# Attention and two feed-forward layers on one core: weight tiles finished a tile earlier, and three edits in the last layer

## The chip, the core and the metric

The kernel runs as one program on one core of a Trainium2 chip. The core has a matrix engine (TensorE, in the profile PE; its weight loads are listed as PEld), a vector engine (VectorE, DVE), a scalar engine (ScalarE, ACT) and GpSimd (POOL). Each runs its own instructions strictly in the order in which they were written, and they meet at semaphores. The sync engine (SP) issues most transfers, also in order; ScalarE issues some of its own. Sixteen DMA engines carry them. SBUF is the on-chip memory, PSUM the memory that TensorE writes to. The metric is the time of one execution in microseconds (us) of the device.

## The reference, cut to what matters

```python
# q, k, v: [4, 8, 768, 64]; per head h: gamma = 1 - 2**(-5-h)
for t in range(768):
    state = gamma * state + k[t] outer v[t]
    y[t]  = q[t] @ state / 8
x  = y as [3072, 512]
h  = x @ w1_in;   g = max(0.01*h, h);             x = g @ w1_out     # first layer,  512 -> 2048 -> 512
h  = x @ w2_in;   g = h * sigmoid(1.702*h);       out = g @ w2_out   # second layer, 512 -> 2048 -> 512
```

The weights arrive as 64-bit floats. All four products are taken from operands that are split in a high and a low part, three matmuls (low x high, high x high, high x low) for each product.

## The kernel before, in words

**Stages.** (1) Attention runs in 24 steps `s` of 128 tokens. (2) The first layer works on six blocks of 512 tokens and 16 slices `m` of the hidden width: `ffn_in(blk, m)` is twelve matmuls of 512 columns, `ffn_out(blk, m)` is twelve too. `ffn_in` of block 0 is woven into the attention steps 4 to 22. After attention, `ffn_in` of block 1 is woven with `ffn_out` of block 0, which catches up by two slices for each `ffn_in` ("the ramp"); from then on the two alternate one to one. (3) The second layer computes each product in seven products of half-size blocks (Strassen's scheme in Winograd's form): `first` runs 32 pairs (block of tokens, slice `q`) of seven products each and writes the gated result to the DRAM tensor `gd`; `second` reads `gd` back, runs seven products of eight slices for each of three blocks of tokens, and turns the results with transposes on TensorE before they go out.

**A first-layer weight tile.** Each call of `work()` moves the tiles of one list (`order`: 16 tiles for `ffn_in`, then 16 for `ffn_out`) one place on: it loads the raw 64-bit words of tile n+2 (`load_raw`, three buffers), converts tile n (`convert`: two ScalarE steps on L137 and L138, four VectorE steps on L139 to L144, an addition on GpSimd on L146), and finishes tile n-1 (`finish`: `split` on L123 and L124, the high part by a copy on ScalarE, the low part by a subtraction on GpSimd, into the tile `home` or `rest`). During attention `work()` runs in steps 2 and 3 and then one step after each step with an `ffn_in`; in the ramp it runs after each `ffn_out` of block 0, and once more before the ramp. Thus tile m is finished in the call just ahead of the matmuls that use it. `ffn_in` and `ffn_out` take the high part in their first two matmuls and the low part in the third.

**What else lies on those engines.** In an attention step VectorE masks the scores (`sm`, L249), updates the state (`st`, L291) and scales the queries (`qs`, L256); GpSimd scales the keys (L260); ScalarE copies the result out (L307). In the ramp `g_split` writes the two parts of the activations of slice n+2 after `ffn_out` of slice n: a ScalarE copy (L123) that waits for the buffer of slice n, and a VectorE subtraction (L124).

**The second layer's buffers.** `first` has a pool of five tiles `g` for results that wait for their store to `gd` (issued by ScalarE, L577); four tiles are written in each pair. As slices of the first weights fall free, `after(q)` has SP load the last layer's weights (`wdo`) into the same place (L839, 1792 KB each). `prepared()` creates `Early`, which has SP load the first eight blocks of `gd` (L694, 256 KB each), three pairs before the end. In `second`, `result()` queues a turn (`turn`, eight transposes on L763, then a ScalarE copy on L767) two ticks later; a tick is one product. For the quarter C22 of the result (`other`, block row 1, column 1) GpSimd first adds two tiles (L778), and its turn uses the same PSUM tile "d" as the turn just before.

Of the kernel before, what the change touches and what calls it, by code (L numbers as in the profile page):

```python
# [13 lines left out]
I32 = mybir.dt.int32  # L14
AF = mybir.ActivationFunctionType
ALU = mybir.AluOpType
# [8 lines left out]
KF = DFF // P  # L25
# [58 lines left out]
def retention_two_ffn(ctx: ExitStack, tc: tile.TileContext, qkv, consts, small, w1i, w1o, w2i, w2o, scratch, out):  # L84
    nc = tc.nc
# [7 lines left out]
    low, low_x = ExitStack(), ExitStack()  # L93
# [21 lines left out]
    later = Later()  # L115
# [3 lines left out]
    xf, raw, conv = {}, {}, {}  # L119
# [11 lines left out]
    def convert(kind, m):  # L131


        t = raw.pop((kind, m))
        low, high = t[:, :, 0], t[:, :, 1]
        a = cv_p.tile([P, 512], U32, tag="a", name="a")
        nc.scalar.activation(out=a.bitcast(F32), in_=high.bitcast(F32), func=AF.Abs)  # L137
        nc.scalar.activation(out=low.bitcast(I32), in_=low, func=AF.Copy, scale=2.0**-29)  # L138
        nc.vector.tensor_scalar(out=high, in0=high, scalar1=0x80000000, scalar2=None, op0=ALU.bitwise_and)  # L139
        nc.vector.tensor_scalar(out=a.bitcast(F32), in0=a.bitcast(F32), scalar1=HW_MIN, scalar2=HW_MAX,  # L140
                                op0=ALU.max, op1=ALU.min)
        nc.vector.tensor_scalar(out=a, in0=a, scalar1=3, scalar2=0x40000000,
                                op0=ALU.logical_shift_left, op1=ALU.bitwise_xor)
        nc.vector.scalar_tensor_tensor(out=a, in0=a, scalar=0x7FFFFFFF, in1=high,  # L144
                                       op0=ALU.bitwise_and, op1=ALU.bitwise_or)
        nc.gpsimd.tensor_tensor(out=a.bitcast(I32), in0=a.bitcast(I32), in1=low.bitcast(I32), op=ALU.add)  # L146
        conv[kind, m] = a, t

    def finish(kind, m):

# [19 lines left out]
    W0 = 4  # L170
# [7 lines left out]
    def work():  # L178

        n = done[0]  # L180
        done[0] += 1
        if n + 2 < len(order):
            kind, m = order[n + 2]
            load_raw(kind, m, w1i if kind == "i" else w1o)
        if n < len(order):
            convert(*order[n])
        if 0 < n <= len(order):
            kind, m = order[n - 1]
            finish(kind, m)

    def ffn_in(blk, m):
        h = ps.tile([P, TB], F32, tag="h", name="h")
# [19 lines left out]
    with ExitStack() as actx:  # L212
# [124 lines left out]
        for s in range(len(steps)):  # L337
            if s == 0:
                keep_warm(6)
            elif s + 1 < len(steps):  # L340
                a_scores(s + 1)
            o = a_out(s)
            if s >= W0 - 2 and done[0] < KF + 1 and (s < W0 or now_in[s - 1]):
                work()
            a_store(s, o)
            if s == 0:
                keep_warm(4)
                a_scores(1)
                keep_warm(6)
            if s + 2 < len(steps):  # L350
                a_decay(s + 2)
            if s + 4 < len(steps):
                a_load(s + 4)
            for m in now_in[s]:
                if m == KF - 1:
                    g_split(seq[0])
                ffn_in(0, m)
# [141 lines left out]
    first2 = KF + LAG  # L499
    g_split(seq[1])  # L500
    work()
    n = 0
    for i in range(KF, len(seq)):
        ffn_in(*seq[i])
# [50 lines left out]
    def first(wt, blocks, g_p, after, prepared):  # L555


        with ExitStack() as c:
# [42 lines left out]
            state = {}  # L601
            for n in range(len(pairs) + 1):
                now = n < len(pairs)
                if n == len(pairs) - 3:
                    prepared()
                cur, old = state.setdefault(n, {}), state.pop(n - 1, None)
                last = first_ = False
# [101 lines left out]
    def second(wt, early):  # L709
        with ExitStack() as c:  # L710
# [41 lines left out]
                                         start=(new and q == 0 and m == 0), stop=(q == NQ - 1 and m == 2),  # L752
                                         skip_group_check=True)

            def result(blk, r, col, t, tag):

                rows = slice((2 * blk + r) * T2, (2 * blk + r + 1) * T2)

# [10 lines left out]
                        out=out[rows].rearrange("(b p) f -> p b f", p=P)[:, :, 2 * col * P : 2 * col * P + 2 * P],  # L769
                        in_=s.rearrange("p b j f -> p b (j f)")))  # L770

                later.at(2, turn)

            kept = {}

            def evacuate(blk, i):
# [15 lines left out]
                elif i == 6:  # L792
# [6 lines left out]

                    def other():  # L800
                        put(k, t, k, e=nc.gpsimd)
                        result(blk, 1, 1, k, "d")

                    later.at(1, other)
                elif i == 3:
# [21 lines left out]
            later.drain()  # L827

    blocks.open(left, 2)
    g_p = pool(left, "g1", 5, "left")  # L830
    for k, i in enumerate(FORMS[4:]):
        blocks.form(0, i, (k, k, k))
    for _ in range(2):
# [77 lines left out]
```

## Time and profile before

| | |
|---|---|
| median of 3 runs | 1297.26 us (1295.88 to 1297.53) |
| the profiled execution | 1292.65 us, of which the span of the profile is 1290.6 us |
| TensorE busy in the span | 1161.7 us, 90% |
| VectorE, ScalarE, GpSimd busy | 655.0, 490.7, 258.0 us |
| TensorE's granted clock, mean of the span | 0.953 of 2.4 GHz |

Times in the views are in us from the span's start. "Idle before" is the time an engine stood still ahead of an instruction, followed by what released it. The granted clock of a stretch is a mean between the two levels 1.2 GHz (0.5) and 2.4 GHz (1.0). A row with "x10" merges ten instructions that follow each other. The end of a matmul is modelled, so neighbouring matmul rows overlap by some tenths of a us.

### The profile page before, as it was taken

To read this page: it belongs to the slowest core of one execution; us is meant where nothing else is said; L and a number is where in the kernel's file an instruction comes from. 1 tells how busy PE (TensorE), PEld (TensorE's weight loads), DVE (VectorE), ACT (ScalarE), POOL (GpSimd) and SP (SyncE) were. 2 spreads that over 40 slices of the span, in tenths; PEclk is the share of its full clock that TensorE was granted. 3 is DMA by queue.
4 is the path that set the end of the run, shared out by engine and by line. 5 is a ranking of instruction groups with operands and counts; after the bars stand their busy time and mean duration, and the time that the engine had idled before them with its cause. 6 is when DMAs were issued, how large, how long until landed. Compare 5 with 4: busy or idle time off the path is not lost.

```text
span 1290.6 us, 16434 instructions
## 1 busy us (share of the span) xinstructions
PE 1161.7 (90%) x6189; PEld 963.5 (75%) x6189; DVE 655.0 (51%) x1034; ACT 490.7 (38%) x823; POOL 258.0 (20%) x269
## 2 busy tenths in 40 slices
PE   8677767656699999999999999999999699999997
PEld 5566555444488888888888889999999687887885
DVE  6344343222235554554454435666574478586683
ACT  2222223222234444444443334344342344444443
POOL 3343231322213333332233301011110000000000
PEclk9898897777799999999999999999999899999999
DMA  9475532111024445444433685343439952623421
GB/s 364 166 267 188 194 121 98 53 61 49 1 100 156 134 147 166 167 151 152 159 127 124 229 338 191 117 153 120 151 106 334 344 188 65 229 66 123 138 66 66
DMA packets 88095, 199.03 MB, mean 154 GB/s; under 512 B 7888, under 2 KB 51920, under 8 KB 82640
## 3 DMA queue, kind: packets, MB, share of 16 engines
q1 hardware_dynamic: 69584, 172.81, 38.8%
q10 hardware_dynamic: 18432, 25.17, 5.4%
q8 instruction: 48, 0.79, 0.2%
q14 instruction: 31, 0.25, 0.1%
HBM read 125.60 MB, written 72.35 MB: 153 GB/s over the span
## 4 chain that ended last, share of the span: by engine, by line
PE 79%; DMA 6%; DVE 5%; POOL 5%; issue 3%; ACT 2%; SPq 0%; POOLq 0%; ACTq 0%; DVEq 0%
PE y L479 22%; PE h L197 21%; PE b L568 6%; PE f L751 5%; PE d L751 5%; PE e L751 4%; PE a L568 4%; DMA gd<-g 4%; PE c L568 4%; PE h L751 3%; POOL home L124 3%; POOL a L146 2%; PE s L245 2%; DVE a L144 1%; DMA in<-qkv 1%
## 5 line engine op out<-in xcount | busy, mean ns | idle before, releaser
L479 PE MATMUL y<-g,home 128*128 128x512 f32 x1008 | 274.4, 424 | 51.8 <-POOL home L124 34.8
L197 PE MATMUL h<-xs,home 128*128 128x512 f32 x1008 | 264.0, 410 | 37.2 <-POOL home L124 37.2
L479 PEld LDWEIGHTS y<-g,home 128*128 128x128 f32 x1008 | 203.1, 204 | 111.4 <-POOL home L124 42.3
L197 PEld LDWEIGHTS h<-xs,home 128*128 128x128 f32 x1008 | 194.6, 196 | 91.2 <-POOL home L124 43.0
L124 DVE TENSOR_TENSOR g<-h,g 128x512 fp32r<-128x512 f32 x96 | 100.2, 1044 | 266.4 <-ACT g L123 266.4
L202 ACT ACTIVATE h<-h 128x512 f32<-128x512 f32 x96 | 57.3, 597 | 233.2 <-PE h L197 231.0
L702 ACT CAST op<-g 128x512 fp32r<-128x512 f32 x168 | 101.5, 621 | 94.3 <-DVE g L729 41.1
L707 DVE TENSOR_TENSOR op<-g,op 128x512 fp32r<-128x512 f32 x168 | 112.4, 688 | 41.9 <-ACT op L702 41.1
L123 ACT CAST g<-h 128x512 fp32r<-128x512 f32 x96 | 59.7, 621 | 182.0 <-PE y L479 181.9
L568 PE MATMUL b<-xf,home 128*128 128x384 f32 x576 | 116.4, 337 | 9.3 <-DVE g L598 9.0
L568 PEld LDWEIGHTS b<-xf,home 128*128 128x128 f32 x576 | 101.9, 189 | 10.0 <-DVE g L598 9.4
L397 POOL TENSOR_TENSOR f<-f,raw 128x512 int32<-128x512 int32 x32 | 41.8, 1306 | 251.9 <-DVE f L393 251.9
L146 POOL TENSOR_TENSOR a<-a,raw 128x512 int32<-128x512 int32 x32 | 44.0, 1376 | 230.6 <-DVE a L144 168.9
L249 DVE TENSOR_TENSOR sm<-s,cst 128x512 f32<-128x512 f32 x48 | 30.9, 685 | 97.7 <-PE s L245 97.7
L568 PE MATMUL a<-xf,home 128*128 128x384 f32 x384 | 77.2, 335 | 2.3 <-ACT b L632 2.3
L568 PE MATMUL c<-xf,home 128*128 128x384 f32 x384 | 76.9, 334 | 0.0
L729 DVE TENSOR_TENSOR g<-g 128x512 f32<-128x512 f32 x96 | 72.5, 755 | 2.3 <-DMA g<-gd 2.3
L403 POOL TENSOR_TENSOR f<-f 128x128 f32<-128x128 f32 x128 | 71.9, 578 | 5.0
L751 PE MATMUL d<-op,home 128*128 128x512 f32 x288 | 70.1, 401 | 1.0 <-DVE op L707 1.0
L751 PE MATMUL e<-op,home 128*128 128x512 f32 x288 | 70.4, 400 | 0.0
L568 PEld LDWEIGHTS a<-xf,home 128*128 128x128 f32 x384 | 67.3, 188 | 3.4 <-ACT b L632 3.3
L751 PE MATMUL f<-op,home 128*128 128x512 f32 x288 | 68.2, 395 | 0.0
(94 smaller groups left out, 1405.6 us busy)
## 6 DMA issues: line engine op xcount, KB each, us to landing
gd<-g ACTq DMA_DIRECT2D x128, 192.0 KB, 2.0
g<-gd SPq DMA_DIRECT2D x96, 256.0 KB, 4.4
in<-qkv SPq DMA_DIRECT2D x21, 1024.0 KB, 6.3
home<-wdi SPq DMA_DIRECT2D x8, 1792.0 KB, 12.8
home<-wdo SPq DMA_DIRECT2D x8, 1792.0 KB, 9.0
raw<-w1i SPq DMA_DIRECT2D x16, 512.0 KB, 6.0
raw<-w1o SPq DMA_DIRECT2D x16, 512.0 KB, 3.2
raw<-w2i SPq DMA_DIRECT2D x32, 256.0 KB, 3.8
```

The costliest lines, as they stand in the source:

```text
L123: nc.scalar.copy(out=hi, in_=src)
L124: (eng or nc.vector).tensor_tensor(out=lo, in0=src, in1=hi.bitcast(F32), op=ALU.subtract)
L146: nc.gpsimd.tensor_tensor(out=a.bitcast(I32), in0=a.bitcast(I32), in1=low.bitcast(I32), op=ALU.add)
L197: nc.tensor.matmul(out=h, lhsT=w[:, a, k], rhs=xs[k][:, c], start=(i == 0), stop=(i == 3 * NP - 1))
L202: nc.scalar.activation(out=t, in_=h, func=AF.Lrelu)
L403: nc.gpsimd.tensor_tensor(out=f[:, o], in0=f[:, a], in1=f[:, b], op=ALU.subtract)
L479: nc.tensor.matmul(out=y[j], lhsT=w[:, a, j * P : j * P + P], rhs=g[:, c], start=(m == 0 and i == 0), stop=(m == KF - 1 and i == 2))
L568: nc.tensor.matmul(out=t, lhsT=w[:, k, a], rhs=x[:, b, k], start=(start and m == 0), stop=(m == 5), skip_group_check=True)
L702: nc.scalar.copy(out=t[:, 0], in_=block_of(raw, *item))
L707: nc.vector.tensor_tensor(out=t[:, 1], in0=block_of(raw, *item), in1=t[:, 0].bitcast(F32), op=ALU.subtract)
L729: nc.vector.tensor_tensor(out=a(*s[0]), in0=a(*s[1]), in1=a(*s[2]), op=s[3])
L751: nc.tensor.matmul(out=t[:, j], lhsT=w[:, j, a], rhs=x[:, b], start=(new and q == 0 and m == 0), stop=(q == NQ - 1 and m == 2), skip_group ...
```

## The change

In the first layer the addition on GpSimd leaves `convert` and becomes `round_in`, which `work()` calls last, behind `finish` of the tile before. `work()` also runs in attention step 4, and twice instead of once before the ramp. In the second layer `prepared()` is called eight pairs before the end instead of three, the pool of `g` tiles has seven buffers instead of five, and the turn of C22 is queued four ticks later instead of two.

```diff
--- before.py
+++ after.py
@@ -143,8 +143,11 @@
                                 op0=ALU.logical_shift_left, op1=ALU.bitwise_xor)
         nc.vector.scalar_tensor_tensor(out=a, in0=a, scalar=0x7FFFFFFF, in1=high,
                                        op0=ALU.bitwise_and, op1=ALU.bitwise_or)
-        nc.gpsimd.tensor_tensor(out=a.bitcast(I32), in0=a.bitcast(I32), in1=low.bitcast(I32), op=ALU.add)
         conv[kind, m] = a, t
+
+    def round_in(kind, m):
+        a, t = conv[kind, m]
+        nc.gpsimd.tensor_tensor(out=a.bitcast(I32), in0=a.bitcast(I32), in1=t[:, :, 0].bitcast(I32), op=ALU.add)
 
     def finish(kind, m):
 
@@ -187,6 +190,8 @@
         if 0 < n <= len(order):
             kind, m = order[n - 1]
             finish(kind, m)
+        if n < len(order):
+            round_in(*order[n])
 
     def ffn_in(blk, m):
         h = ps.tile([P, TB], F32, tag="h", name="h")
@@ -340,7 +345,7 @@
             elif s + 1 < len(steps):
                 a_scores(s + 1)
             o = a_out(s)
-            if s >= W0 - 2 and done[0] < KF + 1 and (s < W0 or now_in[s - 1]):
+            if s >= W0 - 2 and done[0] < KF + 1 and (s <= W0 or now_in[s - 1]):
                 work()
             a_store(s, o)
             if s == 0:
@@ -498,6 +503,7 @@
     preps = [Prep(kind, n) for kind in "io" for n in range(KF)]
     first2 = KF + LAG
     g_split(seq[1])
+    work()
     work()
     n = 0
     for i in range(KF, len(seq)):
@@ -601,7 +607,7 @@
             state = {}
             for n in range(len(pairs) + 1):
                 now = n < len(pairs)
-                if n == len(pairs) - 3:
+                if n == len(pairs) - 8:
                     prepared()
                 cur, old = state.setdefault(n, {}), state.pop(n - 1, None)
                 last = first_ = False
@@ -752,7 +758,7 @@
                                          start=(new and q == 0 and m == 0), stop=(q == NQ - 1 and m == 2),
                                          skip_group_check=True)
 
-            def result(blk, r, col, t, tag):
+            def result(blk, r, col, t, tag, ticks=2):
 
                 rows = slice((2 * blk + r) * T2, (2 * blk + r + 1) * T2)
 
@@ -769,7 +775,7 @@
                         out=out[rows].rearrange("(b p) f -> p b f", p=P)[:, :, 2 * col * P : 2 * col * P + 2 * P],
                         in_=s.rearrange("p b j f -> p b (j f)")))
 
-                later.at(2, turn)
+                later.at(ticks, turn)
 
             kept = {}
 
@@ -799,7 +805,7 @@
 
                     def other():
                         put(k, t, k, e=nc.gpsimd)
-                        result(blk, 1, 1, k, "d")
+                        result(blk, 1, 1, k, "d", 4)
 
                     later.at(1, other)
                 elif i == 3:
@@ -827,7 +833,7 @@
             later.drain()
 
     blocks.open(left, 2)
-    g_p = pool(left, "g1", 5, "left")
+    g_p = pool(left, "g1", 7, "left")
     for k, i in enumerate(FORMS[4:]):
         blocks.form(0, i, (k, k, k))
     for _ in range(2):
```

GpSimd during the attention steps, before: in each call the addition of a tile (L146, `a` is the tile's 32-bit words), then the subtraction that finishes the tile ahead of it (L124, out to `home0`), then the keys of the step (L260).

```order
L146 TENSOR_TENSOR a_536<-a_536,raw_361 128x512
L124 TENSOR_TENSOR home0_60<-a_470,home0_60 128x512
L260 TENSOR_TENSOR in_421<-in_421,smalls_115 128x512
L146 TENSOR_TENSOR a_609<-a_609,raw_468 128x512
L124 TENSOR_TENSOR home0_60<-a_536,home0_60 128x512
L260 TENSOR_TENSOR in_485<-in_485,smalls_115 128x512
```

GpSimd at the same place now (L150 is the addition, L265 the keys):

```order
L124 TENSOR_TENSOR home0_60<-a_420,home0_60 128x512
L150 TENSOR_TENSOR a_482<-a_482,raw_361 128x512
L265 TENSOR_TENSOR in_377<-in_377,smalls_115 128x512
L124 TENSOR_TENSOR home0_60<-a_482,home0_60 128x512
L150 TENSOR_TENSOR a_548<-a_548,raw_418 128x512
L265 TENSOR_TENSOR in_433<-in_433,smalls_115 128x512
```

The subtraction that finishes a tile now stands ahead of the addition of the next tile, and no longer behind it.

SP's queue at the end of `first` and the beginning of `second`, before (`home` from `wdo` are the last layer's weights, `g` from `gd` the blocks that are read back):

```order
L839 DMA home_60<-wdo 128x3584 x4
L694 DMA g<-gd 128x512 x8
L839 DMA home_1649<-wdo 128x3584 x4
L694 DMA g<-gd 128x512 x24
L768 DMA y<-u 128x4x256
```

The same place now:

```order
L700 DMA g<-gd 128x512 x8
L845 DMA home_60<-wdo 128x3584 x4
L845 DMA home_1649<-wdo 128x3584 x4
L700 DMA g<-gd 128x512 x24
L774 DMA y<-u 128x4x256
```

The eight early blocks have moved from the middle of the weight loads to ahead of all of them.

TensorE in `second`, the first products of the form that follows on C22's two operands, before (L751 a product into the PSUM tile `e`, L763 the eight transposes of a turn):

```order
L751 MATMUL e_7780<-op_8087,home0_60 128x512 x6
L763 MATMUL y_8140<-ident_7646,u_8117 128x128 x8
L751 MATMUL e_7780<-op_8097,home0_60 128x512 x6
L763 MATMUL y_8161<-ident_7646,u_7772 128x128 x8
L751 MATMUL e_7780<-op_8107,home0_60 128x512 x6
```

The same place now (L757 and L769):

```order
L757 MATMUL e_7780<-op_8087,home0_60 128x512 x6
L769 MATMUL y_8140<-ident_7646,u_8117 128x128 x8
L757 MATMUL e_7780<-op_8097,home0_60 128x512 x6
L757 MATMUL e_7780<-op_8107,home0_60 128x512 x6
L757 MATMUL e_7780<-op_8121,home1_1649 128x512 x6
L769 MATMUL y_8184<-ident_7646,u_7772 128x128 x8
```

Three products instead of one stand between the two turns.

## Rows read from the trace of the kernel before

**Rows 1.** The page, part 1: busy time of each engine, its share of the span, and its instructions.

```profile
PE 1161.7 (90%) x6189; PEld 963.5 (75%) x6189; DVE 655.0 (51%) x1034; ACT 490.7 (38%) x823; POOL 258.0 (20%) x269
```

**Rows 2.** The view of waits for TensorE, 0 to 380 us: who waited for whom, then the total in us, how often, and the longest.

```profile
PE h L197 <- POOL home L124: 37.2, 12, 4.4
PE y L479 <- POOL home L124: 34.8, 13, 2.9
PE y L479 <- ACT home L123: 16.9, 7, 2.8
PE h L197 <- POOL resti L124: 7.0, 2, 3.7
PE y L479 <- POOL resto L124: 2.8, 1, 2.8
```

**Rows 3.** The table by windows: the window and its length, then for PE, PEld, DVE, ACT and POOL the busy us with the instruction count, then the granted clock of TensorE, the DMA engines' mean busy share and GB/s. The windows are the attention steps from step 5 on, the ramp, the end of `first`, and the one-to-one part of the first layer.

```profile
34.50:201.10 166.60, 123.33 (x1269) 94.80 (x1268) 68.73 (x131) 47.76 (x84) 56.01 (x44) 0.91 0.51 177
201.10:356.80 155.70, 101.11 (x305) 72.55 (x302) 37.97 (x76) 41.10 (x72) 38.77 (x31) 0.76 0.16 54
966.00:1030.00 64.00, 51.66 (x278) 49.28 (x276) 25.75 (x51) 18.06 (x38) 0.50 (x2) 0.92 0.92 332
356.80:748.10 391.30, 391.30 (x1681) 315.33 (x1681) 194.57 (x256) 165.61 (x262) 117.36 (x162) 1.00 0.46 156
```

**Rows 4.** The timeline, 95 to 150 us: start, length, engine, line, operation, operands and count, and in brackets the idle time before and its releaser. First one `ffn_in` of an earlier step, then a mask on VectorE beside an addition on GpSimd, then one whole attention step.

```profile
95.30 4.63 PE L197 MATMUL h<-xs,home 128*128 128x512 f32 x10 [3.48 <-POOL home L124]
...
117.20 1.28 DVE L249 TENSOR_TENSOR sm<-s,cst 128x512 f32<-128x512 f32 x2
...
117.26 1.30 POOL L146 TENSOR_TENSOR a<-a,raw 128x512 int32<-128x512 int32 x1 [8.25 <-DVE a L144]
...
122.37 1.16 PE L245 MATMUL s<-in 64*128 64x128 f32 x16
...
125.97 0.74 PE L197 MATMUL h<-xs,home 128*128 128x512 f32 x2
...
126.35 0.69 DVE L144 SCALAR_TENSOR_TENSOR a<-a,raw 128x512 uint32<-128x512 uint32 x1
...
127.27 1.50 POOL L146 TENSOR_TENSOR a<-a,raw 128x512 int32<-128x512 int32 x1 [5.03 <-DVE a L144]
...
128.74 1.25 POOL L124 TENSOR_TENSOR home<-a,home 128x512 fp32r<-128x512 f32 x1
...
130.05 2.60 PE L197 MATMUL h<-xs,home 128*128 128x512 f32 x10 [3.34 <-POOL home L124]
```

**Rows 5.** The timeline of the ramp, 246 to 270 us: one `ffn_out`, the `work()` behind it, and the next `ffn_out`.

```profile
247.84 4.09 PE L479 MATMUL y<-g,home 128*128 128x512 f32 x10 [2.57 <-POOL home L124]
...
251.97 0.62 ACT L123 CAST g<-h 128x512 fp32r<-128x512 f32 x1 [7.85 <-PE y L479]
...
255.41 1.27 POOL L146 TENSOR_TENSOR a<-a,raw 128x512 int32<-128x512 int32 x1 [7.62 <-ACT h L202]
256.64 1.26 POOL L124 TENSOR_TENSOR home<-a,home 128x512 fp32r<-128x512 f32 x1
...
257.95 4.14 PE L479 MATMUL y<-g,home 128*128 128x512 f32 x10 [2.75 <-POOL home L124]
```

**Rows 6.** The timeline of VectorE and of GpSimd, 430 to 465 us: a subtraction of `g_split` beside an addition on GpSimd, and the same subtraction with GpSimd at rest.

```profile
432.79 1.31 POOL L397 TENSOR_TENSOR f<-f,raw 128x512 int32<-128x512 int32 x1 [7.64 <-DVE f L393]
...
432.98 1.67 DVE L124 TENSOR_TENSOR g<-h,g 128x512 fp32r<-128x512 f32 x1 [0.32 <-ACT g L123]
438.57 0.69 DVE L124 TENSOR_TENSOR g<-h,g 128x512 fp32r<-128x512 f32 x1 [3.93 <-ACT g L123]
```

**Rows 7.** All instructions of line 140, one of the three single-operand VectorE steps of `convert`: shortest, median and longest in ns, and first and last start.

```profile
L140 DVE TENSOR_SCALAR a<-a x32: 411/421/426, 21.9 to 345.4; 128x512 f32<-128x512 f32 x32
```

**Rows 8.** The timeline, 150 to 215 us: the beginning of the ramp.

```profile
206.37 0.62 ACT L123 CAST home<-a 128x512 fp32r<-128x512 f32 x1 [2.83 <-DMA xd<-x]
...
207.04 5.98 PE L479 MATMUL y<-g,home 128*128 128x512 f32 x12 [2.81 <-ACT home L123]
```

**Rows 9.** The timeline, 940 to 1005 and 1005 to 1045 us: SP's weight loads, and TensorE at the end of `first` and the beginning of `second`.

```profile
966.15 24.40 SPq L839 DMA_DIRECT2D home<-wdo  x4
...
1024.09 2.29 PE L568 MATMUL b<-xf,home 128*128 128x384 f32 x6 [9.04 <-DVE g L598]
...
1029.92 10.06 PE L751 MATMUL d<-op,home 128*128 128x512 f32 x42 [0.99 <-DVE op L707]
```

**Rows 10.** The chain of work that ended last, 930 to 1060 us: start, length, what.

```profile
964.04 1.04 PE c L568 x6
...
966.16 8.12 DMA gd<-g
```

**Rows 11.** The view of waits for TensorE, 740 to 1291 us, columns as in Rows 2.

```profile
PE y L763 <- ACT u L767: 7.2, 3, 2.4
```

**Rows 12.** The timeline, 1080 to 1125 us: VectorE behind the addition on GpSimd, and the turn of C22.

```profile
1088.07 2.88 DVE L729 TENSOR_TENSOR g<-g 128x512 f32<-128x512 f32 x1
...
1092.72 1.06 PE L763 MATMUL y<-ident,u 128*128 128x128 f32 x8 [2.38 <-ACT u L767]
```

**Rows 13.** The raw tiles, 0 to 60 us: shortest, median and longest time from a load's issue to its landing.

```profile
DMA to landing us min/median/max: 3.2/6.5/12.3
```

## The prediction

> **What bounds the kernel now.** I read busy time first [rows 1]: TensorE works for 1161.7 of 1290.6 us, so whatever is gained must come out of its idle time or of stretches at the low clock. The waits of TensorE up to 380 us [rows 2] then say where: 37.2 + 7.0 us for the subtraction on GpSimd that finishes an `ffn_in` tile, and 34.8 + 16.9 + 2.8 us for the two parts of an `ffn_out` tile. The table by windows [rows 3] puts them in their stages. The attention steps from step 5 on take 166.6 us at a granted clock of 0.91, with TensorE busy for 123.3, so idle for 43.3, which is nearly all of the 44.2 us above. The ramp takes 155.7 us at 0.76, busy for 101.1, so idle for 54.6: that is 34.8 + 16.9 + 2.8. The one-to-one part has no idle time at clock 1.00; 391.3 us for 1681 matmuls is 2.79 us for each group of twelve.
>
> The timeline shows why. In an attention step [rows 4] scores start at 122.37 and the first two matmuls of `ffn_in` at 125.97; the other ten wait 3.34 us for the low part, which comes at the end of one chain inside the step: last VectorE step of tile n (126.35), addition of tile n (127.27), and only behind it the subtraction of tile n-1 (128.74). The ramp [rows 5] is the same chain behind each `ffn_out`: its end lets ScalarE start at 251.97, the addition runs at 255.41, the subtraction at 256.64, the next ten matmuls at 257.95. From one to the next is 10.11 us, and ten matmuls take 4.1 us where at the full clock they take 2.60 [rows 4, 5].
>
> **First layer, attention steps.** The extra call in step 4 puts the finishing of tile m+1 into the step that uses tile m. The work is the same; TensorE then needs nothing that GpSimd does in the same step. What is late next? Behind the wait TensorE itself needs 125.97 - 122.37 = 3.6 us for attention and 2.8 for `ffn_in`: 6.4 us a step. GpSimd is busy for 56.0 us of the window and VectorE for 68.7 [rows 3], each well below the 112 that remain; that they hold each other up (below) does not reach the masks, which read PSUM: one ran its usual 1.28 us beside an addition [rows 4]. Loads: the window moves 166.6 x 0.51 = 85 us worth of all DMA engines [rows 3], which is less than what is left of the stage; it will be a busy 75 to 80%. So the 43.3 us of idle time go. The clock: 0.91 means 18% of 166.6 = 30 us at half speed; with a busy share of 123.3/166.6 that is 22 us of work that would take 11. Together **54 us**, leaving 112. Counting instead fifteen steps of 6.4, three without `ffn_in` of 3.6 and the last gives about 105, a gain of 61; the lower end is the idle time alone, 43.
>
> **First layer, ramp.** With two calls ahead of it, `ffn_out` of slice n uses a tile that was finished behind slice n-2. Its beginning stays: the first high part waits for the last attention store (2.83 us on ScalarE) and TensorE for that [rows 8]; the first `ffn_out` ends at 207.04 + 5.98 = 213.0, 11.9 us into the ramp. On GpSimd the subtraction of tile n-1 now waits ahead of the addition of tile n, which delays that addition once, here, where nobody is waiting for it yet. After that come nine `ffn_in` and fifteen `ffn_out`. If TensorE bounds them, they are 24 x 2.8 = 67.2 us, and the ramp is 79.1.
>
> But VectorE and GpSimd, which took turns, now overlap. A VectorE subtraction of two SBUF operands that began 0.19 us into an addition on GpSimd took 1.67 us, and with GpSimd at rest 0.69 [rows 6]: it stood until GpSimd was done. One call with its `g_split` is 0.69 + 0.69 us of VectorE steps with two operands [rows 4, 6] and 1.27 + 1.26 of GpSimd [rows 5], 3.91 us, and three single-operand steps of 0.42 [rows 7]. Those never met GpSimd in this trace, all 32 of a line lying within 15 ns. So their price has two ends: nothing, or 1.26 us each call. I take the nearest row, in which a VectorE step on SBUF was held, for them too: 5.17 us a call, 10.3 for the two calls of a round (one `ffn_in`, two `ffn_out`) in which TensorE needs 8.4. The first round still finds finished tiles (8.4), five more take 10.3, and three rounds with one `ffn_out` take 5.6: 8.4 + 51.5 + 16.8 = 76.7, with the beginning 88.6. Gain 155.7 - 88.6 = **67 us**; 76.6 at the one end. At the other, TensorE's waits of about 2 us a round keep its clock down, and the gain is about 50.
>
> The Trainium skill (page "SBUF — State Buffer", section "Who interferes with whom") speaks against this overlap: a VectorE instruction with two SBUF inputs shuts GpSimd's reads out and is shut out by them for a whole instruction, and so does a single-input one such as `tensor_scalar` when it runs in a two-port mode. The first half is what the 1.67 us show; of the second no row here shows anything. By the page the ramp is 88.6 us, without its second half 79.1.
>
> **Second layer, end of `first`.** The last clean product before the weight loads ends at 966.1 [rows 9, 10]; a product takes 1.04. From there six pairs of seven products and three of the last, 45 x 1.04 = 46.8 us, would end at 1012.9; the last product ends at 1026.2 and the products of `second` run without a break from 1029.92. In between a store of `g` took 8.12 us to land [rows 10], in a window with the DMA engines 0.92 busy [rows 3]. A `g` tile is thus held for about 2.1 us (two ticks) + 8.1, the one of four that is gated from a sum about 2 longer, so some 10.7 x 4 / 7.28 = 5.9 tiles are held at once. Five are too few, seven enough. The eight early blocks (2 MB, 6 us at 332 GB/s) move out of this window to a stretch before it, and they no longer stand between weight loads on SP; weights plus stores are then 2.6 MB a pair, about 7.2 us for 7.28. All of it would give 13.3 us. Since the loads still fill the engines and the next blocks queue behind the last weights, I take **10 us**, with ends of 4 and 13.3. VectorE and ScalarE take up the early block 12 ticks after its load, some 12.5 us, against a landing of 8; and the two more tiles cost no time but space.
>
> **Second layer, turn of C22.** TensorE waits 7.2 us in all for ScalarE's copy of the turn before, because both use tile "d" [rows 11]; that copy is late because VectorE stood 2.88 us behind GpSimd's addition [rows 12] and ScalarE behind VectorE. Two more products (2.8 us) now lie in the 2.38 us gap; their operands are prepared three products ahead. The copy and the store of C22 come 2.8 us later and nobody waits for them. **7 us**, at least 4.
>
> **Sum.** 54 + 67 + 10 + 7 = 138 us. From the profiled execution's 1292.65 that leaves 1154.7; the median of the runs shown is 4.6 us higher, so 1297.3 - 138 = **1159 us**.
>
> **The rivals.**
> - *TensorE bounds the ramp too* (the single-operand steps run beside GpSimd): 9.5 us more gain, 1150. For it: their time never varied [rows 7]; against: nothing ever overlapped them.
> - *The clock stays down.* Attention gives 43 us; in the ramp a round is 2 x (0.6 + 4.1) + 2.8 = 12.2, so 11.9 + 6 x 12.2 + 16.8 = 102, a gain of 53. With 10 + 7: 1184. For it: ten matmuls took 4.63 after a wait of 3.48 us [rows 4]; against: after 3.34 us they took 2.60, and the waits left are shorter.
> - *The last layer's edits give nothing*, since loads and stores fill the DMA engines either way and the wait for the copy moves along: 1297 - 121 = 1176.
> - *The tile ahead is not ahead.* The addition, now last on GpSimd, is waited for by the next high part, and TensorE waits for that as long as for the subtraction before. Only the last layer gains: 1280. Against: from addition to the next call's high part lie a whole step of TensorE, 6.4 us, or a round.
> - *Slower: raw words become the bound.* A raw buffer is free after the addition, now the last step of a call, and is loaded for the call three further on. Landing plus some 7 us of conversion must fit in three calls. At a landing of 6.5 us that is 4.5 us a call; to be slower than now (10.1 to 10.2 us a call) a load must land in over 24 us. At 30 a call takes 12.3, 2.1 more than now for 31 calls: 65 us, less 17 from the last layer, 1345. The longest landing at the start, with the engines nearly full, was 12.3 [rows 13].
>
> **How the numbers follow.** The forecast has a chance of 0.52, the TensorE-bound ramp 0.18, the low clock 0.14, the last layer without gain 0.09, the tile that is not ahead (the fifth case) 0.04, slower raw loads 0.03. The bounds of the forecast's terms are 43 to 61, 50 to 76.6, 4 to 13.3 and 4 to 7: not all fall on one side together, so I take 1137 to 1190, which also holds the rivals at 1150, 1176 and 1184. A change of 0.2% is about what a measurement of this kernel can tell from none. Of the fifth case a quarter counts as no change, since its 17 us are open themselves: faster 0.96, same 0.01, slower 0.03.
>
> **What the profile of the changed kernel would show.** The attention steps take 6.4 to 7 us each, `ffn_in` is one row of twelve matmuls, and the stage ends near 147 us. In the ramp the rounds are near 10.3 us with VectorE steps of 1.5 us and more beside GpSimd, or near 8.4 with none; the granted clock is above 0.95 after its first `ffn_out`. At the end of `first` TensorE's 9.0 us wait is gone and `second` follows within 4 us. The row of 7.2 us is gone. What would make the prediction wrong: TensorE still waiting for GpSimd in the attention steps; the keys or queries of a step late because its load landed late; the clock at 0.76 in the ramp.

## The result, and the profile after

| | before | after |
|---|---|---|
| median | 1297.39 us (1295.88 to 1300.90, 4 runs) | 1140.45 us (1140.12 to 1140.88, 4 runs) |
| the profiled execution, its span | 1292.65, 1290.6 us | 1140.88, 1139.1 us |
| granted clock, mean of the span | 0.953 | 0.995 |

The ratio is 0.8787 (95% interval 0.8769 to 0.8805): 156.9 us less by the medians, 151.5 by the two profiled spans. The profiled run of before lay 4.7 us below its median, which is most of the difference between these two sums. By stages, from the start of the same TensorE instruction in both traces:

| stage | before, us | after, us | gain | predicted |
|---|---|---|---|---|
| up to the end of the attention steps | 201.1 | 140.7 | 60.4 | 54 |
| ramp | 155.7 | 80.6 | 75.1 | 67 |
| from there to the first product of `second` behind the wait | 673.1 | 664.3 | 8.8 | 10 |
| the rest | 260.7 | 253.5 | 7.2 | 7 |

From `ffn_in` on, line numbers of the changed kernel are 5 or 6 higher (`ffn_in` L202, `ffn_out` L484, product of `first` L574, of `second` L757); the addition is L150. Busy time of each engine, answering to [rows 1]: TensorE works 46 us less for the same work, the rest of the gain was idle time.

```profile
PE 1115.6 (98%) x6188; PEld 939.2 (82%) x6189; DVE 694.6 (61%) x1034; ACT 492.3 (43%) x823; POOL 269.1 (24%) x269
```

The table by windows, answering to [rows 3] line by line (attention steps, ramp, end of `first`, one-to-one part):

```profile
33.40:140.70 107.30, 107.30 (x1270) 86.88 (x1269) 82.32 (x130) 46.36 (x81) 58.96 (x44) 1.00 0.78 281
140.70:221.30 80.60, 74.54 (x303) 58.13 (x302) 63.32 (x76) 42.63 (x72) 46.70 (x31) 0.96 0.31 105
823.00:890.00 67.00, 60.72 (x335) 58.89 (x334) 35.09 (x67) 24.51 (x50) 0.50 (x2) 0.97 0.90 325
221.30:612.70 391.40, 391.40 (x1682) 315.36 (x1681) 194.36 (x256) 165.80 (x262) 117.33 (x162) 1.00 0.46 156
```

The attention steps have no idle time left, at clock 1.00. Their busy time fell from 123.33 to 107.30 us with one instruction's difference in count; in the ramp it fell from 101.11 to 74.54. Most of that is the clock: in the trace of before TensorE is busy at the lower level for 27.4 us of the attention steps and 56.0 of the ramp. The same work takes half as long at the upper one (twelve matmuls of `ffn_out` 5.98 us at the lower level [rows 8], 2.96 at the upper), which is 13.7 and 28.0 us less; the ramp still has 6.8 us at the lower level. VectorE's busy time rose by 13.6 and 25.4 us, although it does the same work: it now stands behind GpSimd. The one-to-one part is untouched.

TensorE's waits up to 260 us, the counterpart of [rows 2]. The 37.2 and 7.0 us at `ffn_in` are gone, the 34.8 at `ffn_out` are 2.4, and the wait for ScalarE is paid once:

```profile
PE y L484 <- ACT home L123: 3.7, 1, 3.7
PE y L484 <- POOL home L124: 2.4, 5, 0.6
```

The ramp, the counterpart of [rows 5]: TensorE, VectorE and GpSimd from 172 to 182 us in one timeline (ScalarE's rows are left out). Between the first matmuls of two `ffn_in` (170.81 and 179.96) lie 9.15 us, in the next rounds 9.08, 9.09 and 9.10.

```profile
176.35 1.66 DVE L144 SCALAR_TENSOR_TENSOR a<-a,raw 128x512 uint32<-128x512 uint32 x1
177.51 2.61 PE L484 MATMUL y<-g,home 128*128 128x512 f32 x10 [0.47 <-POOL home L124]
177.93 0.68 DVE L124 TENSOR_TENSOR g<-h,g 128x512 fp32r<-128x512 f32 x1
178.08 1.69 POOL L150 TENSOR_TENSOR a<-a,raw 128x512 int32<-128x512 int32 x1 [0.63 <-DVE a L144]
178.53 1.53 DVE L139 TENSOR_SCALAR raw<-raw 128x512 uint32<-128x512 uint32 x1
...
179.98 0.42 DVE L140 TENSOR_SCALAR a<-a 128x512 f32<-128x512 f32 x1
180.43 0.43 DVE L142 TENSOR_SCALAR a<-a 128x512 uint32<-128x512 uint32 x1
180.51 1.50 POOL L124 TENSOR_TENSOR home<-a,home 128x512 fp32r<-128x512 f32 x1 [0.73 <-ACT home L123]
180.89 1.66 DVE L144 SCALAR_TENSOR_TENSOR a<-a,raw 128x512 uint32<-128x512 uint32 x1
```

VectorE goes from step to step without a gap, 4.54 us from one L144 to the next, and is held twice in it: L139 ends 0.3 us behind the addition, L144 0.5 us behind the subtraction. L139 has one tensor operand, takes 0.42 us when free and 1.53 here. The addition in turn lasts 1.69 us, not 1.3, since it met VectorE's L124.

**A wait that was not there before.** At the end of `first` the 9.0 us of [rows 9] are gone, but TensorE now stands ahead of the second group of products. The chain that ended last, 870 to 890 us:

```profile
874.55 9.22 DMA home<-wdo
...
883.85 0.33 ACTq L583
...
884.22 0.63 ACT op L708
...
884.87 0.70 DVE op L713
...
885.62 4.47 PE d L757 x12
```

The timeline of the same place:

```profile
878.67 5.51 ACTq L583 DMA_DIRECT2D gd<-g  x4
884.22 3.22 ACT L708 CAST op<-g 128x512 fp32r<-128x512 f32 x6 [5.07 <-DMA home<-wdo]
885.62 4.71 PE L757 MATMUL d<-op,home 128*128 128x512 f32 x13 [5.60 <-DVE op L713]
```

ScalarE issues the stores of `g`; the row of 5.51 us merges four of them. The third is out at 880.2. The last is not issued until an earlier weight block (issued at 874.55) has landed at 883.77, with which it shares no data, and the high parts of `second` are queued behind it: 3.6 us of standing still. In place of 9.0 + 1.0 us TensorE waits 0.7 + 5.6, and then its first 42 matmuls (seven products) take 11.3 us at a granted clock of 0.86, where before they took 9.9 at 1.00 (second line):

```profile
885.60:896.90 11.30, 11.28 (x42) 9.05 (x43) 8.26 (x14) 4.94 (x9) 0.00 (x0) 0.86 0.89 305
1029.90:1039.80 9.90, 9.88 (x42) 8.00 (x43) 7.59 (x13) 4.43 (x9) 0.00 (x0) 1.00 1.00 359
```

The turn of C22 has no wait any more: the row of [rows 11] is gone, although VectorE still stands behind the addition as in [rows 12] (timeline, 942 to 952 us):

```profile
945.18 2.87 DVE L735 TENSOR_TENSOR g<-g 128x512 f32<-128x512 f32 x1
...
950.22 1.03 PE L769 MATMUL y<-ident,u 128*128 128x128 f32 x8
```

### The profile page after: what moved, and what is told of

It is laid out like the page before. It is cut to its first block, busy times and chain, and to the rows that moved or that the text cites. A ratio compares the mean times of both kernels' runs of the same rounds, so it can differ in the third digit from the quotient of the medians.

```text
span 1139.1 us, 16412 instructions
## 1 busy us (share of the span) xinstructions
PE 1115.6 (98%) x6188; PEld 939.2 (82%) x6189; DVE 694.6 (61%) x1034; ACT 492.3 (43%) x823; POOL 269.1 (24%) x269
## 4 chain that ended last, share of the span: by engine, by line
PE 92%; DMA 3%; DVE 2%; issue 1%; POOL 0%; ACT 0%; SPq 0%; ACTq 0%; POOLq 0%; DVEq 0%
PE h L202 23%; PE y L484 22%; PE b L574 9%; PE e L757 6%; PE d L757 6%; PE f L757 6%; PE a L574 6%; PE c L574 6%; PE h L757 3%; PE s L250 2%; PE o L287 2%; PE o L293 2%; DMA in<-qkv 1%; PE kv L281 1%; PE y L769 1%
## 5 line engine op out<-in xcount | busy, mean ns | idle before, releaser
L484 PE MATMUL y<-g,home 128*128 128x512 f32 x1008 | 250.0, 398 | 6.1 <-ACT home L123 3.7
L202 PE MATMUL h<-xs,home 128*128 128x512 f32 x1008 | 251.1, 397 | 0.0
L484 PEld LDWEIGHTS y<-g,home 128*128 128x128 f32 x1008 | 190.1, 189 | 54.5 <-POOL home L124 4.5
L202 PEld LDWEIGHTS h<-xs,home 128*128 128x128 f32 x1008 | 188.7, 188 | 47.4 <-issue 2.2
L124 DVE TENSOR_TENSOR g<-h,g 128x512 fp32r<-128x512 f32 x96 | 100.8, 1050 | 162.5 <-ACT g L123 162.5
L574 PE MATMUL b<-xf,home 128*128 128x384 f32 x576 | 115.3, 334 | 1.2 <-DVE g L604 0.7
L574 PEld LDWEIGHTS b<-xf,home 128*128 128x128 f32 x576 | 101.1, 188 | 1.8 <-DVE g L604 1.0
L574 PE MATMUL a<-xf,home 128*128 128x384 f32 x384 | 76.8, 334 | 0.0
L574 PE MATMUL c<-xf,home 128*128 128x384 f32 x384 | 76.8, 334 | 0.0
L757 PE MATMUL d<-op,home 128*128 128x512 f32 x288 | 70.3, 402 | 5.6 <-DVE op L713 5.6
L757 PEld LDWEIGHTS d<-op,home 128*128 128x128 f32 x288 | 54.9, 192 | 19.2 <-DVE op L713 6.0
L757 PE MATMUL e<-op,home 128*128 128x512 f32 x288 | 70.2, 398 | 0.0
L757 PE MATMUL f<-op,home 128*128 128x512 f32 x288 | 68.2, 395 | 0.0
L574 PEld LDWEIGHTS a<-xf,home 128*128 128x128 f32 x384 | 67.5, 188 | 0.1
L574 PEld LDWEIGHTS c<-xf,home 128*128 128x128 f32 x384 | 67.5, 188 | 0.0
```

The lines of the kernel that those rows point to most:

```text
L124: (eng or nc.vector).tensor_tensor(out=lo, in0=src, in1=hi.bitcast(F32), op=ALU.subtract)
L202: nc.tensor.matmul(out=h, lhsT=w[:, a, k], rhs=xs[k][:, c], start=(i == 0), stop=(i == 3 * NP - 1))
L484: nc.tensor.matmul(out=y[j], lhsT=w[:, a, j * P : j * P + P], rhs=g[:, c], start=(m == 0 and i == 0), stop=(m == KF - 1 and i == 2))
L574: nc.tensor.matmul(out=t, lhsT=w[:, k, a], rhs=x[:, b, k], start=(start and m == 0), stop=(m == 5), skip_group_check=True)
L757: nc.tensor.matmul(out=t[:, j], lhsT=w[:, j, a], rhs=x[:, b], start=(new and q == 0 and m == 0), stop=(q == NQ - 1 and m == 2), skip_group ...
```

## Experiments

The theory behind the prediction has four parts: TensorE's subtraction wait ends because tiles are a step ahead; in the ramp what is left is that VectorE and GpSimd exclude each other; the end of `first` wanted buffers; the turn only had to be later. All diffs are against the changed kernel, all ratios against the kernel before. Its own time, run again beside the last experiments, was 1140.51 us (ratio 0.8777, 0.8759 to 0.8795).

**Parts ahead, addition in its old place.**

```diff
 def convert(kind, m):
...
+        nc.gpsimd.tensor_tensor(out=a.bitcast(I32), in0=a.bitcast(I32), in1=low.bitcast(I32), op=ALU.add)
         conv[kind, m] = a, t
 def round_in(kind, m):
...
-        nc.gpsimd.tensor_tensor(out=a.bitcast(I32), in0=a.bitcast(I32), in1=t[:, :, 0].bitcast(I32), op=ALU.add)
+        pass
```

> The parts a tile ahead are kept, but GpSimd's addition stands again right behind the scaling of the same call, so that VectorE's subtraction again waits for both. Theory (each part alone takes the subtraction off TensorE's path in the attention steps, and in the ramp it is the tile ahead that counts): attention within 3 us of the changed kernel's 107.3, ramp 0 to 5 us longer, 1140 to 1147 us in all. Rival (the order of the addition is what carries the gain): the attention steps lose 10 us or more and the whole is above 1150 us.

Measured 1156.58 us, ratio 0.8904 (0.8882 to 0.8927). The attention steps are as in the changed kernel (107.2 us), as the theory has it, but the ramp takes 95.2 us, 14.7 more, three times what I allowed. The view of waits, 141 to 235 us, names a wait that no theory had:

```profile
ACT a L137 <- POOL home L124: 24.3, 12, 2.7
```

ScalarE starts a call (L137, which writes a new tile `a`) only when GpSimd has finished the subtraction of the call before. There are two buffers of `a`. With the addition of tile n ahead of the subtraction of tile n-1, the older buffer is released behind the newer tile's addition, which needs the whole VectorE chain; ScalarE, VectorE, addition and subtraction then run one after the other, 172.93 to 178.85 = 5.9 us a call. The timeline of ScalarE:

```profile
172.93 0.66 ACT L137 ACTIVATE a<-raw 128x512 f32<-128x512 f32 x1 [2.58 <-POOL home L124]
...
178.85 0.66 ACT L137 ACTIVATE a<-raw 128x512 f32<-128x512 f32 x1 [2.64 <-POOL home L124]
```

In this kernel VectorE's steps hardly meet GpSimd's, and L139 keeps its length; in the changed kernel it doesn't. All 32 instructions of the line (shortest, median and longest in ns, first and last start), here and then in the changed kernel:

```profile
L139 DVE TENSOR_SCALAR raw<-raw x32: 414/429/549, 21.7 to 225.4; 128x512 uint32<-128x512 uint32 x32
```

```profile
L139 DVE TENSOR_SCALAR raw<-raw x32: 411/1256/1547, 21.5 to 210.4; 128x512 uint32<-128x512 uint32 x32
```

**The same with three buffers of `a`** (and two of the raw words):

```diff
-        t = cv_p.tile([P, 512, 2], U32, tag="raw", name="raw", bufs=3)
+        t = cv_p.tile([P, 512, 2], U32, tag="raw", name="raw", bufs=2)
...
-        a = cv_p.tile([P, 512], U32, tag="a", name="a")
+        a = cv_p.tile([P, 512], U32, tag="a", name="a", bufs=3)
```

> As the kernel with parts ahead and the old order of the addition, but with three buffers in place of two for the converted word, tile a (and two in place of three for the raw words, to make room). Theory (with the addition ahead of the subtraction on GpSimd, the older tile's buffer comes free only behind the newer tile's addition, so that ScalarE's start, VectorE's steps and both GpSimd steps of a call run one after the other, 5.9 us a call): with a third buffer the ramp goes from 95 us to 80 to 86 and the whole from 1156.6 to 1141 to 1147 us. Rival (VectorE's wait for GpSimd in the order itself, or late raw words): the ramp stays at 92 us or more, 1153 us or more in all.

Measured 1154.06 us (0.8882, 0.8865 to 0.8899), ramp 88.6: between theory and rival. ScalarE's wait is gone, so the buffer was real and cost 6.6 of the 14.7 us at the least. A round is now 10.24 us (188.58 to 198.82), and TensorE waits 1.5 us in each for the subtraction, which stands right behind the addition on GpSimd:

```profile
183.53 1.31 POOL L146 TENSOR_TENSOR a<-a,raw 128x512 int32<-128x512 int32 x1 [2.04 <-DVE a L144]
184.80 1.27 POOL L124 TENSOR_TENSOR home<-a,home 128x512 fp32r<-128x512 f32 x1
...
186.13 2.61 PE L484 MATMUL y<-g,home 128*128 128x512 f32 x10 [1.52 <-POOL home L124]
```

That is the order itself: ScalarE never stands still ahead of L137 here, so neither late raw words nor the buffer of `a` hold a call. Five rounds (167.67 to 219.29) take 51.6 us, where the changed kernel takes 44.8 (162.41 to 207.23): 6.8 of the 8 us that are left. The other 1.2 lies ahead of them and is not the order: the first high part of an `ffn_out` tile waits 6.05 us for the last attention store, and 3.73 in the changed kernel. The attention steps end 4 us later too. There the two raw buffers show: up to 155 us SP, which issues the loads and stores of attention in the same queue, waits 83.2 us for a raw buffer to come free, and 38.7 in the kernel with the same order and three; TensorE waits 2.9 us for loads.

**Later addition, calls as before.**

```diff
-            if s >= W0 - 2 and done[0] < KF + 1 and (s <= W0 or now_in[s - 1]):
+            if s >= W0 - 2 and done[0] < KF + 1 and (s < W0 or now_in[s - 1]):
...
-    work()
     work()
```

> The later addition is kept, but the calls are made as in the kernel before: none is a tile ahead, and the call that stood ahead of the ramp is back. Theory (the same as of the run beside it): attention within 3 us of 107.3, because the subtraction is done about 3.7 us into a step and wanted at about 4.1; the ramp's rounds wait again for a whole tile, about 101 us in place of 80.6, 1160 us in all. Rival one (the tile ahead carries everything): near 1275 us. Rival two (the order carries everything): near 1141 us.

Measured 1177.43 us (0.9069, 0.9043 to 0.9096). The attention steps end at 143.1, 2.4 us later: here too one part suffices. The ramp takes 113.0 us, 32.5 more and not 20. A round is 13.9 us (172.18 to 186.10), because TensorE waits for both parts of a tile that is finished in the call just ahead; the granted clock from 158 us to the end of the ramp is 0.90. Of the 32.5 us, 2.5 are the last attention store again, for which the first high part waits 6.24 us:

```profile
166.89 0.73 PE L484 MATMUL y<-g,home 128*128 128x512 f32 x2 [2.36 <-ACT home L123]
168.25 4.10 PE L484 MATMUL y<-g,home 128*128 128x512 f32 x10 [0.62 <-POOL home L124]
```

**Fewer single-operand steps.** The three statements of VectorE's L139, L140 and L142 are kept for the `ffn_in` tiles only, so this kernel leaves out a part of the `ffn_out` weights' conversion:

```diff
-        nc.vector.tensor_scalar(out=high, in0=high, scalar1=0x80000000, scalar2=None, op0=ALU.bitwise_and)
...
+        if kind == "i":
+            nc.vector.tensor_scalar(out=high, in0=high, scalar1=0x80000000, scalar2=None, op0=ALU.bitwise_and)
...
```

> Leaves out VectorE's three single-operand steps for the weight tiles of the second product of the first layer (the sign bit, the clamp, the shift), so a part of those weights' conversion isn't done. Theory (such a step and GpSimd's exclude each other, so that a pair of calls in the ramp is as long as the sum of VectorE's and GpSimd's work): a call of the second product's tiles is some 1.3 us shorter; the four rounds that stand on that sum go from 9.1 to about 8.4 us, where TensorE is the bound, 1137 to 1138 us in all. Rival (single-operand steps run beside GpSimd and are only stretched in the records): no change, 1140 to 1141 us.

Measured 1139.06 us (0.8766, 0.8740 to 0.8792), which alone isn't clear of the changed kernel; but the ramp is 3.0 us shorter, 77.5. Its rounds are at TensorE's own pace, 8.40 us (170.30, 178.70, 187.10, 195.50), with no wait inside. The whole is only 1.4 us lower, since the first products of `second` came 1.4 us later; that place varies by more between two profiles of one kernel (673.2 and 675.4 us from the end of the ramp to the first `e` product, with the last store moved). That the steps exclude each other is read from the rows of L139 above; this run shows that what a round takes over TensorE's 8.4 us goes with these steps.

```profile
187.10 2.96 PE L203 MATMUL h<-xs,home 128*128 128x512 f32 x12
189.90 5.76 PE L485 MATMUL y<-g,home 128*128 128x512 f32 x24
```

**The first layer's edits alone.** The second layer is as before:

```diff
-                if n == len(pairs) - 8:
+                if n == len(pairs) - 3:
...
-                        result(blk, 1, 1, k, "d", 4)
+                        result(blk, 1, 1, k, "d")
...
-    g_p = pool(left, "g1", 7, "left")
+    g_p = pool(left, "g1", 5, "left")
```

> Only the edits of the first layer; the second layer's blocks, buffers and turn are as in the kernel before. Theory (the two halves of the change add up): 1140.5 plus the 8.9 us of the end of the gated half and the 7.2 us of the turn, 1156 to 1157 us. Rival (the transfers that the shorter first layer moves together cost or give something): off that by more than 3 us.

Measured 1159.15 us (0.8925, 0.8905 to 0.8946), 2 to 3 us above the theory: the halves add up but for the clock, which I had left out. TensorE waits 2.4 us at the turn three times, and in two of the three windows there the clock is 0.89.

**The second layer's edits one by one.** Of the diff just shown the first part alone (late blocks):

> The second layer's weight blocks are called three pairs ahead again, with the seven buffers kept. Theory (the two buffers carry most of the gain at the end of the gated half, the earlier reading the smaller part): 2 to 5 us slower than the changed kernel, 1142 to 1146 us. Rival (the earlier reading carries all of it): 1149 us.

the third alone (five buffers; the pool is that of the results that wait for their store):

> Five buffers for the reread operands in place of seven, with the blocks still called eight pairs ahead. Theory (the buffers carry most): 4 to 9 us slower, 1145 to 1149 us. Rival (the earlier reading carries all): 1140 to 1141 us.

and the second alone (early turn):

> C22 of the second layer is turned two ticks behind its sum again. Theory (the turn's wait for ScalarE and VectorE comes back as a whole, since nothing else of the change stands there): 7.2 us slower, 1147 to 1148 us. Rival (what the wait cost is absorbed behind it): less than 2 us slower.

Measured: late blocks 1145.95 us (0.8803, 0.8782 to 0.8823), five buffers 1147.84 (0.8823, 0.8805 to 0.8841), early turn 1151.71 (0.8856, 0.8835 to 0.8877). From the end of the ramp to the first `e` product it is 675.8 us in the changed kernel, 680.8 with late blocks, 682.6 with five buffers, and 684.9 with both and the early turn (which comes behind it). So the buffers alone give 4.1 and the earlier blocks alone 2.3 of the 9.1 us, and the rest needs both. That the buffers are worth more is not shown: 1.8 us is less than the 2.2 by which two profiles of one kernel differ here. The turn's wait came back exactly (7.2, 3, 2.4 in the view of waits), but the span is 9.8 us longer. Of the other 2.6, 1.3 is the third turn's clock: by windows from the first `e` products to the next group, early turn and then the changed kernel, TensorE's busy time is 14.41 against 13.10 us. The rest, 1.4, lies ahead of the first `e`:

```profile
1112.20:1129.00 16.80, 14.41 (x64) 11.73 (x63) 10.27 (x12) 8.12 (x12) 2.61 (x1) 0.90 0.19 63
```

```profile
1106.40:1119.50 13.10, 13.10 (x65) 10.56 (x64) 10.21 (x12) 7.75 (x12) 2.71 (x1) 1.00 0.24 81
```

**The last store on SP's queue.**

```diff
-                store = lambda t: nc.scalar.dma_start(out=gd[f * NQ + q][:, cols], in_=t)
+                queue = nc.sync if (n, r, f) == (len(pairs) - 1, 1, 0) else nc.scalar
+                store = lambda t: queue.dma_start(out=gd[f * NQ + q][:, cols], in_=t)
```

> The last store of a gated operand is issued from SP's queue and not from ScalarE's, where in the changed kernel it stands 5.5 us behind the landing of a weight block, with ScalarE's high parts of the next product queued behind it. Theory (that wait holds ScalarE, ScalarE holds VectorE's low part, and this holds TensorE for 5.6 us): TensorE's wait shrinks by 2.5 to 3.7 us, 1137 to 1138 us. Rival (the reads of the operands would end it as late anyway): 1140 to 1141 us.

> The last store of a gated operand on SP's queue, once more, beside the changed kernel on one chip. Theory: 2.5 to 3.7 us faster than the changed kernel, about 1137 us. Rival: the same within 1 us.

> The changed kernel itself, beside the run with the last store moved, on one chip. Theory (the store behind a weight block costs 3.2 us): it is 2.5 to 3.7 us slower than that kernel. Rival (their difference so far is one of two chips): the same within 1 us.

Measured 1138.62 us (0.8753, 0.8732 to 0.8773), and again 1138.47 (0.8763, 0.8741 to 0.8784) beside 1140.51 on the same chip. The medians are 1.8 and 2.0 us lower, but the intervals overlap: that it is faster is likely, not shown. What the trace does show is that ScalarE was held by that store: its high parts start at 880.67, no longer at 884.22. And the store goes out no earlier from the other queue:

```profile
883.62 0.32 SPq L584 DMA_DIRECT2D gd<-g  x1
884.03 12.79 SPq L701 DMA_DIRECT2D g<-gd  x14
```

It was issued at 883.85 from ScalarE's. The trace's records of semaphores (counters on which an engine waits) say why. SP and ScalarE take eight of them in turn for their transfers; in both kernels this store waits for, and then raises, the one that the weight block raises as it lands, and it goes out within 0.1 us of that. So the queue of issue decides only who stands still. TensorE's wait is split in two, since the blocks that are read back come no earlier than in the changed kernel (their first load is issued at 884.03, there at 884.02) and now end the second wait:

```profile
880.67 3.75 ACT L709 CAST op<-g 128x512 fp32r<-128x512 f32 x7 [1.05 <-DVE g L592]
882.07 8.67 PE L758 MATMUL d<-op,home 128*128 128x512 f32 x36 [1.58 <-DVE op L714]
...
890.65 0.69 DVE L736 TENSOR_TENSOR g<-g 128x512 f32<-128x512 f32 x1 [5.63 <-DMA g<-gd]
...
892.00 1.20 PE L758 MATMUL d<-op,home 128*128 128x512 f32 x4 [1.26 <-DVE op L714]
```

In the second run the two waits were 2.5 and 2.3 us, against 5.6 in one. Theory and rival were each half right.

## Why the prediction held, and where it was off

The likeliest case came about, with the two large terms too small: 138 us predicted, 151.5 measured between the spans. The measured 1140.45 us lies 19 us under the forecast and close to the lower end of the range, 13.5 from the terms and most of the rest from taking a gain of the profiled run off a median that lies 4.7 us above it. By the time alone one would have picked the rival of a TensorE-bound ramp, at 1150; it is the length of the rounds that decides against it.

- **Attention, 54 predicted, 60.4 measured.** The idle time went, as said (43.3 us). The term that was too small is the clock: I took the low clock to be spread over busy and idle time alike, 22 us of work that would take 11. Busy time fell by 16.0 us. The low stretches of this window add up to 30.7 us, and TensorE was busy for 27.4 of them, 89% and not the 74% of the whole stage; that makes 13.7, and where the other 2.3 come from is open. The last 1.1 us is an earlier beginning of step 5. The step is 6.6 us (107.3 for the stage), near the count of 6.4 that gave the upper bound of 61. That count was summed wrongly: fifteen steps of 6.4 and three of 3.6 are 106.8 us before the last one, not 105 with it, so its gain is under 60. The masks, which I took to be out of GpSimd's way, are: 0.68 us in the median in both kernels (the 1.28 us that I read is a row of two).
- **Ramp, 67 predicted, 75.1 measured.** The beginning was sized rightly (the first `ffn_out` ends 12.7 us in, predicted 11.9), and so was the kind of bound. Two things were off. The price of a call was the sum of all its VectorE and GpSimd steps, 5.17 us; it is 4.55. A held step ends 0.3 or 0.5 us behind GpSimd's, less than its free length, and only two of a call's five VectorE steps are held. And four rounds of 9.1 stand on it where I had five of 10.3; the one ahead of them still found finished tiles (162.41 to 170.81, 8.4 us). Up to the same last `ffn_out` the ramp is 83.3 us against 88.6 predicted. The other 2.8 us is my own slip: the 155.7 us of [rows 3] end ahead of that `ffn_out`, the 88.6 behind it.
- **The rival of a TensorE-bound ramp** is refuted for this kernel and shown to be the next bound: without the single-operand steps the rounds are 8.40 us and the stage 77.5. The Trainium skill (page "SBUF — State Buffer", section "Who interferes with whom") says that single-input steps such as `tensor_scalar` in a two-port mode shut GpSimd out and are shut out. The trace of before could not show it; now L139 reads 1256 ns in the median where it overlaps and 429 where it hardly does, so trace and page agree that such steps and GpSimd exclude each other. That these ran in a two-port mode, the page's condition, no view shows.
- **End of `first`, 10 predicted, 8.8 measured**, 7.4 if the slower first products behind it are counted. The wait named is gone; that the next limit would be ScalarE behind its own store was not foreseen, and the sign I had named, `second` within 4 us, did not come: its seventh matmul starts 7.2 us behind its first. The prediction counted the buffers and the earlier blocks as one gain; apart they give 4.1 and 2.3 of 9.1 us, so neither is enough.
- **Turn, 7 predicted, 8.6 measured**: from the first `e` product to the end it is 250.8 us before and 242.2 after. 7.2 is the waits, the rest the clock behind one of them. The table's last line shows 7.2 because the 1.4 us behind the new wait are set against it.
- **The rivals of a low clock, of a last layer without gain, of a tile that isn't ahead and of late raw words** didn't occur: the attention steps stand at 1.00, 16 us came from the last layer, and TensorE's waits in the ramp add up to 6 us.
- **A point on which I was wrong without harm:** I credited the ramp to the tile ahead. Either part undone costs the ramp 14.7 or 32.5 us. The order of two GpSimd steps also sets when a buffer is free.

What stays open: how much of the old-order kernel's 95 us would remain with a third buffer of `a` and all three raw buffers, which wasn't run; and what the last store would gain with a semaphore of its own, which no run gives it.

## What to carry to other kernels

When a chain of engines inside a step ends in a wait, count first how many steps ahead its result could be, and then look at what else the order on the last engine releases: two instructions exchanged on GpSimd freed a buffer as well as a result. Where low clock and idle time come together, look at what the low stretches hold: here 89% of them was work, not the 74% of the whole stage. When a wait is removed next to a queue of transfers, look at which engine issues them: one store, held by the landing of an unrelated block, kept everything behind it in ScalarE's queue.

## What the hardware showed that I had not expected

- A VectorE step held by GpSimd ends 0.3 to 0.5 us behind GpSimd's instruction, where its free length is 0.42 or 0.69; the cost of taking turns is 4.55 us a call and not the sum of 5.17. GpSimd is held as well: its addition takes 1.69 us behind a VectorE step, 1.3 alone.
- Short waits can cost the clock half as much again. With the turn early, TensorE waits 2.4 us three times a run; two of these windows stay at 1.00 and the third is at 0.90, 16.8 us for the work of 15.5. In the run of the first layer's edits alone it was two of three.
- An issue on ScalarE's queue stood 3.6 us until another queue's transfer had landed, and everything ScalarE had to do stood with it (the 5.5 us in my expectation was the length of a row of four issues). From SP's queue the same store waited for the same landing.
